# A kernel on one core of a Trainium2 chip: block products of batch 1 in another order, and a last tile in two halves

## The chip, the cores and the metric

The program runs on one core of one Trainium2 chip. The core has five engines that run side by side, each working through its own queue in order: TensorE (PE, matmuls into PSUM), VectorE (DVE), ScalarE (ACT), GpSimd (POOL) and SyncE (SP, which here issues the transfers). PE's granted clock over the profiled execution was 0.994 of full speed. The metric is the device time of one execution in microseconds; the figure given is the median of three runs.

## What is computed

The reference chains three blocks. Attention over clusters makes `x`; a block with a Fourier mix over both axes follows; then a gated block with a convolution along the tokens.

```python
# attention, per batch and head: scores only where q and k fall to the same centroid
x = np.ascontiguousarray(attn_out.transpose(0, 2, 1, 3)).reshape(B, S, H * D)   # 2 x 768 x 512
X = np.fft.fft(np.fft.fft(x, axis=1), axis=2)
u = x + np.real(X)
un = (u - mu) / np.sqrt(var + 1e-06)
u = u + np.maximum(un @ w_ch1, 0.0) @ w_ch2            # 512 -> 2048 -> 512
h = np.maximum(u @ w_in, 0.0)                          # 512 -> 1024
gate = 1.0 / (1.0 + np.exp(-conv_out(h)))              # 3 taps along the tokens
out = h * gate @ w_out                                 # 1024 -> 512
```

The change lies in `np.maximum(un @ w_ch1, 0.0) @ w_ch2` for batch 1, at the start of the gated block, and at the very last output tile.

## The kernel before

The program has three stages: attention with the Fourier mix of batch 0 woven in (to about 225 us), the first feed-forward block (16 weight blocks `f` for each of two batches `g`, to about 497 us), and the gated block (8 weight blocks for each batch, to the end). Every product of the feed-forward blocks is made of three fp16 matmuls (`pass3`, L491 to L494: high by high, high by low, low by high), so each operand is kept as a high and a low half: ACT converts to the high half, DVE subtracts it from the source to get the low half. `general` is the slower variant of the whole program; the run takes the other one, so only lines with `general` false matter.

**Downs.** `downs` (L1834) is a generator: for weight block `f` it multiplies the activated block `h` into six PSUM accumulators, one tile of 128 tokens (three matmuls of 512 columns) per step.

**Batch 1's ups.** For batch 1 the up-products of two weight blocks (a pair `p`) are made by seven block products instead of eight (`ups`, L1729), each of six matmuls of 384 columns: p1, p6, p2, p7, p5, p4, p3 in this order. They need sums of weight quarters, which `weight_sums(p)` (L1714) makes: six additions and subtractions on POOL into the one-buffer tile `sv`, then a conversion on ACT (L1726) and a subtraction on DVE (L1727) into a two-buffer tile. The products' results are added up out of PSUM: ACT copies p1 to `u1` (L1760); DVE adds p6 to give `u2` (L1763), p2 to give half a row `c1` (L1766), p7 to give `u3` (L1769); p5 is copied by ACT to SBUF (L1773), added by DVE to `u3` (L1775, high half of `c2`) and by POOL to `u2`, giving `u4` (L1777); p4 gives the low half of `c2` (L1779), p3 with `u4` the high half of `c1` (L1782). `keep` applies the relu and splits a row in two halves (L1754 on ACT, L1755 on DVE) for a later `downs`.

**Banks.** All these products, and the side work below, are written to the two-buffer PSUM ring `up`: a product can start only when the bank of the last but one has been read out.

**Turns.** `in_turn` lays tiles of downs (d) and products (u) out on PE by a string of letters; a pair's products are spread over two blocks `f`, four in the even one and three in the odd one. The side generator (`gate_in(0)`, L1860) makes batch 0's input of the gated block: per step four transposes, ACT copies (L1906) and a DVE subtraction (L1907), which give the bank back. It is advanced inside `downs` after the tile numbers in `when`.

**Loads.** `load_w` (L728) brings a weight block as raw 64-bit words (a two-buffer tile, 1 MB, issued by SP at L732) and converts it: three DVE steps in a chain, `ops[0]`, `ops[1]`, `ops[3]` (L710, L711, L713), two on ACT (L712, L716), and then squares for the scale on ACT (L759). The gated block's eight blocks b0 to b7 are loaded in this way during batch 1, into slots that batch 1's own blocks leave. `scales("b")` needs all their sums (L772, `sumsb`) before `split_16` (L1681 on ACT, L1682 on DVE) can make fp16 halves of them.

**The order of the queues.** A scheduler lays each engine's instructions out ahead of time: among those that its own model holds ready, the one written first in the program goes first, so one that is ready early may stand ahead of one written earlier. `with tc.issue_after(i):` puts what is issued inside behind instruction `i` in that engine's queue, without a wait for its end.

**The end.** For the last weight block, each of the six output tiles is scaled by DVE or ACT in turn and stored by SP (L1853 to L1857).

Of the kernel before, what the change touches and what calls it, by code (L numbers as in the profile page):

```python
# [449 lines left out]
def tile_net(ctx, tc, qk, v, cen, w12, w34, conv, dft, odd, out, general):  # L450
# [277 lines left out]
    def load_w(k, f):  # L728
# [15 lines left out]
        with tc.issue_after(last_op[0]) if last_op else nullcontext():  # L744
            ops = from64(w, raw, None if general else sums[:, 64 + f:65 + f])
            for op in ops[0:2] + ops[3:4] if not general else ops:
                i = op()
            last_op[:] = [i.ins]
# [963 lines left out]
    sums_w = {}  # L1712

    def weight_sums(p):  # L1714
        k = hp.tile([128, 2048], F32, tag="sv", bufs=1, name=f"sv{p}").rearrange("p (s c n) -> p s c n", s=8, c=2)
        v, a1, a2 = k[:, 0:4], k[:, 4:6], k[:, 6:8]
        for f, d in ((2 * p, a2), (2 * p + 1, a1)):
            w = w32["a", f].rearrange("p (a i h c n) -> p a i h c n", a=2, i=2, h=2, c=2)
            G.tensor_add(d, w[:, 0, 0], w[:, 1, 0])  # L1719
        G.tensor_add(v[:, 0], a2[:, 0], a2[:, 1])  # L1720
        G.tensor_sub(v[:, 1], v[:, 0], a1[:, 0])
        G.tensor_sub(v[:, 2], a1[:, 0], a2[:, 0])
        G.tensor_sub(v[:, 3], a1[:, 1], v[:, 1])
        t = hp.tile([128, 1024], F32, tag="src", bufs=2, name=f"s16{p}").bitcast(F16)
        t = sums_w[p] = t.rearrange("p (a s c n) -> p a s c n", a=2, s=4, c=2)
        A.copy(t[:, 0], v)  # L1726
        V.tensor_sub(t[:, 1], v, t[:, 0])  # L1727

    def ups(p):  # L1729
# [30 lines left out]
        A.copy(u1, o)  # L1760
# [5 lines left out]
        V.tensor_add(c1[:, lo], u1, product("p2", own(0, 1), 1))  # L1766
        yield
        u3 = piece("u3")
        V.tensor_add(u3, u2, product("p7", of_sum(2), 5))  # L1769
        yield  # L1770
        o = product("p5", of_sum(0), 3)
        p5 = piece("p5")
        A.copy(p5, o)  # L1773
        c2 = row(1)
        V.tensor_add(c2[:, hi], u3, o)  # L1775
        u4 = piece("u4")
        G.tensor_add(u4, u2, p5)  # L1777
        yield
        V.tensor_add(c2[:, lo], u3, product("p4", own(1, 1), 6))  # L1779
        keep(c2, 2 * p)  # L1780
        yield
        V.tensor_add(c1[:, hi], u4, product("p3", of_sum(3), 2))  # L1782
# [51 lines left out]
    def downs(s, g, f, side, when=(2,)):  # L1834
# [4 lines left out]
        for t in range(NT):  # L1839
# [4 lines left out]
            if f == last:  # L1844
# [6 lines left out]
                else:  # L1851
                    y = gps[0].tile([128, 512], F32, tag="y", bufs=6, name=f"y{g}{t}")
                    if t % 2:  # L1853
                        V.tensor_scalar(y, acc[s, g][t], yscs[g][:, t:t + 1], None, ALU.mult)
                    else:
                        A.activation(y, acc[s, g][t], AF.Copy, scale=yscs[g][:, t:t + 1])
# [98 lines left out]
    for g in range(B):  # L1955
        for f in range(16):
# [3 lines left out]
            if not general and g == 0 and f > 13:  # L1960
                weight_sums(f - 14)
            if not general and g and f % 2 == 0 and f < 12:
                weight_sums(f // 2 + 2)
            if (g, f) == (B - 1, 15):
                next(side, None)
            steps = downs(0, g, f, side, (1, 4) if g == 0 and f else (2,))
            if not pairs:
                for _ in steps:
                    pass
            elif g == 0:  # L1970
                in_turn(steps, ups(0), iter("ududduuduudud"))
            elif f % 2:
                in_turn(steps, *made)
            else:
                made = (ups(f // 2 + 1), iter("ududdududduddudduddudd")) if f < 14 else ((), repeat("d"))
                in_turn(steps, *made)
            for i in A_LOADS[f] if g == 0 else ():
# [4 lines left out]
            if g == 1 and f in B_LOADS:  # L1982
                load_w("b", B_LOADS.index(f))
# [14 lines left out]
            for i in {13: (0,), 14: (1,), 15: (2,)}.get(f, ()) if g == 1 else ():  # L1998
# [4 lines left out]
    for n in range(-3, 8 * B):  # L2003
        if n + 3 < 8 * B:
            mlp2_up((n + 3) // 8, (n + 3) % 8)
        if 0 <= n + 2 < 8 * B:
# [91 lines left out]
```

## Time and profile before

| | us |
|---|---|
| median of three runs | 638.51 |
| lowest and highest | 636.48, 639.45 |
| the profiled execution | 637.55 |
| its span, first to last instruction | 635.8 |
| PE busy | 602.3 |
| DVE busy | 509.4 |
| ACT busy | 438.2 |
| POOL busy | 236.0 |

The profile shows one execution. The 1.75 us between its time and its span lie outside the first and last instruction. A busy share is a mean over stages; the rows that tell what waits for what come from the waits, which put every idle time of an engine down to the instruction that ended it, and from the timeline, which lists instructions in order with the idle time ahead of them in brackets.

### The profile page before, as it was taken

To read this page: it belongs to the slowest core of one execution; us is meant where nothing else is said; L and a number is where in the kernel's file an instruction comes from. 1 tells how busy PE (TensorE), PEld (TensorE's weight loads), DVE (VectorE), ACT (ScalarE), POOL (GpSimd) and SP (SyncE) were. 2 spreads that over 40 slices of the span, in tenths; PEclk is the share of its full clock that TensorE was granted. 3 is DMA by queue.
4 is the path that set the end of the run, shared out by engine and by line. 5 is a ranking of instruction groups with operands and counts; after the bars stand their busy time and mean duration, and the time that the engine had idled before them with its cause. 6 is when DMAs were issued, how large, how long until landed. Compare 5 with 4: busy or idle time off the path is not lost.

```text
span 635.8 us, 11958 instructions
## 1 busy us (share of the span) xinstructions
PE 602.3 (95%) x4707; PEld 366.7 (58%) x4707; DVE 509.4 (80%) x833; ACT 438.2 (69%) x744; POOL 236.0 (37%) x193
## 2 busy tenths in 40 slices
PE   8899899999999999999999898989999999999995
PEld 4476577676877755566555454544455555555542
DVE  5989979899898898878798298888643799877663
ACT  6788889996889777774678236677511968867652
POOL 4978877875797300001005616445501000000000
PEclk9999999999999999999999999999999999999998
DMA  4776754541310414430432301314200003245202
GB/s 151 206 183 210 210 152 126 155 126 46 100 42 9 195 65 134 142 124 1 147 119 71 129 2 66 133 51 154 96 1 1 1 0 101 101 147 170 81 1 105
DMA packets 21945, 64.41 MB, mean 101 GB/s; under 512 B 7126, under 2 KB 8822, under 8 KB 19064
## 3 DMA queue, kind: packets, MB, share of 16 engines
q1 hardware_dynamic: 20872, 59.81, 29.6%
q0 software_dynamic: 1008, 3.75, 1.9%
q8 instruction: 39, 0.64, 0.4%
q14 instruction: 26, 0.21, 0.1%
HBM read 49.59 MB, written 4.89 MB: 86 GB/s over the span
## 4 chain that ended last, share of the span: by engine, by line
PE 56%; DVE 25%; ACT 12%; issue 3%; DMA 2%; POOL 1%; DVEq 0%; ACTq 0%
PE acc L494 6%; PE acc L493 6%; PE acc L492 6%; PE av L1325 5%; PE t L1269 4%; DVE m6all L1218 4%; PE t L1271 4%; PE s L1209 3%; PE av L1318 2%; PE u L492 2%; PE u L493 2%; PE u L494 2%; PE p L492 2%; DVE wb L711 2%; PE p L493 2%
## 5 line engine op out<-in xcount | busy, mean ns | idle before, releaser
L1306 POOL TENSOR_TENSOR p<-p,p 128x768 f16<-128x768 f32 x61 | 108.1, 1781 | 39.1 <-DVE p L1294 15.0
L1218 DVE TENSOR_REDUCE m6all<-s 128x1 f32<-128x768 f32 x96 | 90.0, 949 | 9.8 <-PE s L1209 7.5
L1278 ACT ACTIVATE p<-t,cbias 128x768 f32<-128x768 f32 x93 | 83.2, 897 | 14.2 <-PE t L1271 13.5
L492 PE MATMUL acc<-wa,h 128*128 128x512 f16 x186 | 70.6, 379 | 0.0
L493 PE MATMUL acc<-wa,h 128*128 128x512 f16 x186 | 70.5, 379 | 0.0
L494 PE MATMUL acc<-wa,h 128*128 128x512 f16 x186 | 70.5, 379 | 0.0
L1325 PEld LDWEIGHTS <-p 128*128 128x128 f16 x1458 | 55.0, 98 | 11.9 <-issue 3.1
L1325 PE MATMUL av<-V,p 128*128 128x65 f16 x1458 | 58.2, 194 | 0.0
L1269 PE MATMUL t<-X 97*128 97x384 f16 x192 | 47.5, 328 | 4.7 <-DVE m6all L1218 2.4
L1209 PE MATMUL s<-X 80*128 80x384 f16 x192 | 46.9, 328 | 5.0 <-DVE eq L1014 3.0
L1296 ACT CAST p<-p 128x768 f16<-128x768 f32 x60 | 49.5, 825 | 0.9
L674 POOL TENSOR_TENSOR rs<-rs,half 128x1 f32<-128x1 f32 x12 | 9.2, 768 | 105.9 <-DVE rs L669 99.7
L1271 PE MATMUL t<-Y 128*128 128x384 f16 x192 | 47.2, 327 | 0.0
L1719 POOL TENSOR_TENSOR sv<-wa 128x512 f32<-128x512 f16 x16 | 26.2, 1657 | 51.7 <-DVE s L1727 37.0
L492 PE MATMUL up<-un,wa 128*128 128x384 f16 x128 | 41.7, 326 | 3.5 <-DVE h L1708 1.9
L492 PE MATMUL u<-x,wb 128*128 128x384 f16 x128 | 41.7, 326 | 1.2 <-DVE h L1803 1.1
L494 PE MATMUL up<-un,wa 128*128 128x384 f16 x128 | 41.7, 326 | 0.0
L493 PE MATMUL up<-un,wa 128*128 128x384 f16 x128 | 41.7, 326 | 0.0
L494 PE MATMUL u<-x,wb 128*128 128x384 f16 x128 | 41.7, 326 | 0.0
L493 PE MATMUL u<-x,wb 128*128 128x384 f16 x128 | 41.7, 326 | 0.0
L493 PE MATMUL acc<-wb,gH 128*128 128x512 f16 x96 | 36.4, 379 | 0.0
L492 PE MATMUL acc<-wb,gH 128*128 128x512 f16 x96 | 36.4, 379 | 0.0
(411 smaller groups left out, 1521.8 us busy)
## 6 DMA issues: line engine op xcount, KB each, us to landing
rawa<-w SPq DMA_DIRECT2D x14, 1024.0 KB
rawb<-w SPq DMA_DIRECT2D x8, 1024.0 KB
heads<-qk SPq DMA_DIRECT2D x8, 768.0 KB
raw<-qk SPq DMA_DIRECT2D x7, 768.0 KB
Y<-G SPq DMA_DIRECT2D x27, 192.0 KB
vraw<-v SPq DMA_DIRECT2D x8, 384.0 KB
heads<-v SPq DMA_DIRECT2D x8, 384.0 KB
out<-y SPq DMA_DIRECT2D x12, 256.0 KB
```

Of the source, the lines that this page charges most:

```text
L492: T.matmul(o, sH, mH, start=start, stop=False)
L493: T.matmul(o, sH, mL, start=False, stop=False)
L494: T.matmul(o, sL, mH, start=False, stop=stop)
L1209: T.matmul(t[:, c, 0:384], X[0:80, 0, sl], X[0:80, 1, 384 * c:384 * c + 384], start=True, stop=True)
L1218: V.tensor_reduce(m6s[h][:, i:i + 1], t[:, :, 0:384], AX.XY, ALU.max, negate=True)
L1269: T.matmul(t[:, c, 0:384], X[0:rx, 1, sl], X[0:rx, 0, 384 * c:384 * c + 384], start=True, stop=False)
L1271: T.matmul(t[:, c, 0:384], Y[0:ry, k, sl], Y[0:ry, q, 384 * c:384 * c + 384], start=False, stop=True)
L1278: A.activation(p, t[:, :, 0:384], AF.Exp, bias=cbias[:, 0:1], scale=0.125 if general else 0.125 / QK_SCALE ** 2)
L1296: A.copy(p16[:, 0], p32s[n])
L1306: eng.tensor_sub(p16[:, 1], p, p16[:, 0])
L1325: T.matmul(o, p16[:, k, 128 * j:128 * j + 128], v16[:, i, h % 2, 65 * part:65 * part + 65], start=(i + j + k + part == 0), stop=(i == 5), ...
L1719: G.tensor_add(d, w[:, 0, 0], w[:, 1, 0])
```

## The change

In short: `weight_sums` loses its conversion and subtraction, which become `split_sums` and are queued behind additions of the pair that is running; both are called behind the downs of a block instead of ahead of them, by two tables of block numbers (16 g + f). The three DVE steps of a load are queued behind `u3`, the high half of `c2` and its low half, by the marks that `ups` had left last when the load was written. The ACT copy of p5, `u4` and POOL's addition are gone; DVE adds p5 to `u2` in place. `u3` is kept in the high half of `c1`. The turns of pair 0 and the side step's places change. The third weight block of the gated block is split behind its first up-product. The last output tile is scaled in two halves, one by DVE and one by ACT, and stored by two issues, one from SP and one from ACT.

```diff
@@ load_w
-            for op in ops[0:2] + ops[3:4] if not general else ops:
-                i = op()
+            if general:
+                for op in ops:
+                    i = op()
+            else:
+                for op, m in ((ops[0], "u3"), (ops[1], "c2"), (ops[3], "c2lo")):
+                    with tc.issue_after(marks[m]):
+                        i = op()
@@ weight sums
-    sums_w = {}
+    sums_w, marks = {}, {}
+    SUM_SPLITS = {14: (0,), 15: (1,), **{2 * p + 12: (p,) for p in range(2, 8)}}
+    WEIGHT_SUMS = {12: (0,), 14: (1,), 15: (2,), **{2 * p + 10: (p,) for p in range(3, 8)}}
+
+    def split_sums(p):
+        v = sums_w[p][:, 0:4]
         t = hp.tile([128, 1024], F32, tag="src", bufs=2, name=f"s16{p}").bitcast(F16)
         t = sums_w[p] = t.rearrange("p (a s c n) -> p a s c n", a=2, s=4, c=2)
-        A.copy(t[:, 0], v)
-        V.tensor_sub(t[:, 1], v, t[:, 0])
+        with tc.issue_after(marks["u1"]) if p == 1 else nullcontext():
+            A.copy(t[:, 0], v)
+        with tc.issue_after(marks["c1"]) if marks else nullcontext():
+            V.tensor_sub(t[:, 1], v, t[:, 0])
@@ ups
-        u3 = piece("u3")
-        V.tensor_add(u3, u2, product("p7", of_sum(2), 5))
+        u3 = c1[:, hi]
+        marks["u3"] = V.tensor_add(u3, u2, product("p7", of_sum(2), 5)).ins
         yield
         o = product("p5", of_sum(0), 3)
-        p5 = piece("p5")
-        A.copy(p5, o)
         c2 = row(1)
-        V.tensor_add(c2[:, hi], u3, o)
-        u4 = piece("u4")
-        G.tensor_add(u4, u2, p5)
+        marks["c2"] = V.tensor_add(c2[:, hi], u3, o).ins
+        V.tensor_add(u2, u2, o)
         yield
-        V.tensor_add(c2[:, lo], u3, product("p4", own(1, 1), 6))
+        marks["c2lo"] = V.tensor_add(c2[:, lo], u3, product("p4", own(1, 1), 6)).ins
         keep(c2, 2 * p)
         yield
-        V.tensor_add(c1[:, hi], u4, product("p3", of_sum(3), 2))
+        V.tensor_add(c1[:, hi], u2, product("p3", of_sum(3), 2))
@@ the last output tile
+                    if (g, t) == (B - 1, NT - 1) and not general:
+                        V.tensor_scalar(y[:, 0:256], acc[s, g][t][:, 0:256], yscs[g][:, t:t + 1], None, ALU.mult)
+                        A.activation(y[:, 256:512], acc[s, g][t][:, 256:512], AF.Copy, scale=yscs[g][:, t:t + 1])
+                        nc.sync.dma_start(out=out[g, 128 * t:128 * t + 128, 0:256], in_=y[:, 0:256])
+                        nc.scalar.dma_start(out=out[g, 128 * t:128 * t + 128, 256:512], in_=y[:, 256:512])
+                        yield
+                        continue
@@ the loop over g and f
-            if not general and g == 0 and f > 13:
-                weight_sums(f - 14)
-            if not general and g and f % 2 == 0 and f < 12:
-                weight_sums(f // 2 + 2)
-            steps = downs(0, g, f, side, (1, 4) if g == 0 and f else (2,))
+            when = (1, 4) if g == 0 and f else (2,) if general or not g else (3,) if f % 2 else (5,)
+            steps = downs(0, g, f, side, when)
-                in_turn(steps, ups(0), iter("ududduuduudud"))
+                in_turn(steps, ups(0), iter("uduududuududd"))
+            for p in SUM_SPLITS.get(16 * g + f, ()) if not general else ():
+                split_sums(p)
+            for p in WEIGHT_SUMS.get(16 * g + f, ()) if not general else ():
+                weight_sums(p)
-            for i in {13: (0,), 14: (1,), 15: (2,)}.get(f, ()) if g == 1 else ():
+            for i in {13: (0,), 14: (1,), 15: (2,) if general else ()}.get(f, ()) if g == 1 else ():
@@ the gated block's loop
+        if n == -3 and not general:
+            ws_b[2] = split_16(wbp[0], "b", 2)
```

## Rows read from the trace of the kernel before

**Rows 1.** The page, part 1: busy us, share of the span, instructions.

```profile
PE 602.3 (95%) x4707; PEld 366.7 (58%) x4707; DVE 509.4 (80%) x833; ACT 438.2 (69%) x744; POOL 236.0 (37%) x193
```

**Rows 2.** PE's waits, 345 to 490 us: total us, times, longest.

```profile
PE p L492 <- DVE u L1763: 4.5, 3, 1.8
PE p L492 <- DVE x L1907: 2.4, 3, 1.5
PE up L492 <- DVE h L1708: 1.9, 1, 1.9
```

**Rows 3.** PE's waits, 490 to 520 us.

```profile
PE u L492 <- DVE h L1803: 1.1, 1, 1.1
```

**Rows 4.** DVE's timeline, pairs 2 to 4: start, duration, instruction, [idle before].

```profile
394.36 2.18 DVE L711 SCALAR_TENSOR_TENSOR wb<-rawb,wb 128x1024 int32<-128x1024 int32 x1
396.46 0.54 DVE L1763 TENSOR_TENSOR u<-u,p 128x384 f32<-128x384 f32 x1
...
402.49 1.23 DVE L711 SCALAR_TENSOR_TENSOR wb<-rawb,wb 128x1024 int32<-128x1024 int32 x1
...
407.92 0.68 DVE L1907 TENSOR_TENSOR x<-xT,x 128x512 f16<-128x512 f32 x1
...
430.43 0.69 DVE L710 TENSOR_SCALAR wb<-rawb 128x1024 int32<-128x1024 int32 x1 [0.50 <-DMA rawb<-w]
...
436.34 1.19 DVE L710 TENSOR_SCALAR wb<-rawb 128x1024 int32<-128x1024 int32 x1 [0.30 <-PE acc L494]
```

**Rows 5.** POOL's timeline, first two weight sums for pairs 2 and 4.

```profile
358.38 2.26 POOL L1719 TENSOR_TENSOR sv<-wa 128x512 f32<-128x512 f16 x2 [2.42 <-DVE s L1727]
...
393.65 3.90 POOL L1719 TENSOR_TENSOR sv<-wa 128x512 f32<-128x512 f16 x2 [6.06 <-DVE s L1727]
```

**Rows 6.** ACT's timeline, pair 1's conversion.

```profile
355.99 1.05 ACT L1726 CAST s<-sv 128x1024 f16<-128x1024 f32 x1 [4.72 <-POOL sv L1723]
```

**Rows 7.** Stretches, pairs 2 and 7: length, busy PE, PEld, DVE, ACT, POOL.

```profile
390.00:408.20 18.20, 15.96 (x89) 8.61 (x88) 15.43 (x18) 12.44 (x25) 8.92 (x7) 1.00 0.33 116
...
475.00:490.00 15.00, 15.00 (x84) 8.09 (x82) 5.16 (x8) 2.92 (x5) 0.99 (x1) 1.00 0.01 1
```

**Rows 8.** PE's timeline, end of pair 2.

```profile
405.45 0.60 PE L1904 MATMUL xT<-ident,U 128*128 128x128 f32 x4
405.89 0.38 PE L492 MATMUL acc<-wa,h 128*128 128x512 f16 x1
...
406.53 0.33 PE L492 MATMUL p<-un,s 128*128 128x384 f16 x1
...
407.51 0.38 PE L492 MATMUL acc<-wa,h 128*128 128x512 f16 x1
...
408.80 0.33 PE L492 MATMUL p<-un,wa 128*128 128x384 f16 x1
```

**Rows 9.** Groups by line: busy us, mean ns | idle before.

```profile
L1777 POOL TENSOR_TENSOR u<-u,p 128x384 f32<-128x384 f32 x8 | 10.0, 1254 | 43.8 <-ACT p L1773 43.7
...
L1769 DVE TENSOR_TENSOR u<-u,p 128x384 f32<-128x384 f32 x8 | 4.4, 551 | 4.2 <-PE p L494 4.2
```

**Rows 10.** The chain that ended last, in order of time: a raw transfer.

```profile
425.68 4.73 DMA rawb<-w
```

**Rows 11.** ACT's timeline, the last square of b6.

```profile
443.75 0.19 ACT L759 ACTIVATION_READ_ACCUMULATOR rawb<-wb 128x1 f32 x1
```

**Rows 12.** ACT's and DVE's timelines, start of the gated block.

```profile
500.69 1.93 ACT L1681 ACTIVATE wb<-wb,scb 128x512 f16<-128x512 f32 x3
...
500.86 1.40 DVE L1682 SCALAR_TENSOR_TENSOR wb<-wb,scb,wb 128x512 f16<-128x512 f32 x2
502.19 0.55 DVE L1809 SCALAR_TENSOR_TENSOR h<-u,x 128x384 f32<-128x384 f32 x1
```

**Rows 13.** DVE's and SP's timelines, the end.

```profile
628.69 0.75 DVE L1854 TENSOR_SCALAR y<-acc,ysc 128x512 f32<-128x512 f32 x1 [0.54 <-PE acc L494]
...
626.16 3.64 SPq L1857 DMA_DIRECT2D out<-y  x6
```

More of the change, by code (lines that the diff above doesn't have):

```diff
@@ L1710, in mlp1_up @@
             ws[0, g, f + 1] = split_16(hp, "a", f + 1)
-    sums_w = {}
+    sums_w, marks = {}, {}
+    SUM_SPLITS = {14: (0,), 15: (1,), **{2 * p + 12: (p,) for p in range(2, 8)}}
+    WEIGHT_SUMS = {12: (0,), 14: (1,), 15: (2,), **{2 * p + 10: (p,) for p in range(3, 8)}}
     def weight_sums(p):
-        k = hp.tile([128, 2048], F32, tag="sv", bufs=1, name=f"sv{p}").rearrange("p (s c n) -> p s c n", s=8, c=2)
+        k = sums_w[p] = hp.tile([128, 2048], F32, tag="sv", bufs=1, name=f"sv{p}").rearrange("p (s c n) -> p s c n", s=8, c=2)
         v, a1, a2 = k[:, 0:4], k[:, 4:6], k[:, 6:8]
@@ L1759, in ups @@
         u1 = piece("u1")
-        A.copy(u1, o)
+        marks["u1"] = A.copy(u1, o).ins
         yield
@@ L1765, in ups @@
         c1 = row(0)
-        V.tensor_add(c1[:, lo], u1, product("p2", own(0, 1), 1))
+        marks["c1"] = V.tensor_add(c1[:, lo], u1, product("p2", own(0, 1), 1)).ins
         yield
-        u3 = piece("u3")
-        V.tensor_add(u3, u2, product("p7", of_sum(2), 5))
+        u3 = c1[:, hi]
+        marks["u3"] = V.tensor_add(u3, u2, product("p7", of_sum(2), 5)).ins
         yield
         o = product("p5", of_sum(0), 3)
-        p5 = piece("p5")
-        A.copy(p5, o)
         c2 = row(1)
-        V.tensor_add(c2[:, hi], u3, o)
-        u4 = piece("u4")
-        G.tensor_add(u4, u2, p5)
+        marks["c2"] = V.tensor_add(c2[:, hi], u3, o).ins
+        V.tensor_add(u2, u2, o)
         yield
-        V.tensor_add(c2[:, lo], u3, product("p4", own(1, 1), 6))
+        marks["c2lo"] = V.tensor_add(c2[:, lo], u3, product("p4", own(1, 1), 6)).ins
         keep(c2, 2 * p)
         yield
-        V.tensor_add(c1[:, hi], u4, product("p3", of_sum(3), 2))
+        V.tensor_add(c1[:, hi], u2, product("p3", of_sum(3), 2))
         keep(c1, 2 * p + 1)
@@ L1982, in tile_net @@
             if g == 1 and f in B_LOADS:
-                load_w("b", B_LOADS.index(f))
+                for i in range(8):
+                    if B_LOADS[i] == f:
+                        load_w("b", i)
             if (g, f) == (0, 14):
```

## The prediction

> **What bounds the kernel now.** I read the page's busy times first: TensorE (PE) is busy 602.3 of 635.8 us [rows 1], so an edit on another engine pays only where it ends a wait of PE. I then read PE's waits over the stage that the diff touches, from the last up-products of batch 0's loop to the end of batch 1's pairs (345 to 490 us) [rows 2]. There are seven, all on a PSUM bank of the two-buffer `up` ring that an engine has not read out: 4.5 us in three for the addition to `u2` (L1763), 2.4 us in three for the low half of a transposed block (L1907), 1.9 us in one for L1708. Together 8.8 us. After 490 us there is one more, 1.1 us [rows 3]. That is all the change can win on PE, besides the tail behind the last matmul.
>
> The timelines show why they arise. In pair 2, VectorE (DVE) starts L711 of a weight load at 394.36 and holds it 2.18 us; `u2`'s addition is behind it at 396.46, and p2, whose bank it frees, waits with PE idle: the longest of the three, 1.8 us [rows 2, 4]. L711 took 1.23 us at 402.49, with GpSimd (POOL) idle for most of it; the 2.18 us lie beside POOL's first two sums, which took 3.90 us there and 2.26 at 358.38 [rows 4, 5]. So two engines slow each other, and DVE's order puts the slowed instruction in front of an addition that PE needs. The 1.9 us wait is another order: ScalarE (ACT) sits 4.72 us at L1726 until POOL has summed pair 1's weights [rows 6], with the reading out of `up` queued behind it.
>
> DVE is not short of time on average: 15.43 of 18.20 us in pair 2, 5.16 of 15.00 in pair 7, which has neither loads nor weight sums [rows 7].
>
> **Clock of a pair.** From PE's starts in pair 2: a tile of three downs is 0.65 us (407.51 to 408.80 for two), a product 0.98 (406.53 to 407.51), a block of transposes 0.44 (405.45 to 405.89, where the next downs stand) [rows 8]. Twelve tiles, seven products and two blocks are 15.5 us. In the new turns, counted from p1's start: p1 0, p6 1.6, p2 3.9, p7 5.5, first transposes 7.8, p5 8.2, p4 10.5, second transposes 12.8, p3 13.2, next p1 15.5.
>
> **The change part by part.**
> *Weight sums and splits.* For pair 1 the ACT copy and DVE subtraction go behind `u1` and `c1` of pair 0, whose operands PE makes; L1708 then waits for PE alone. The 1.9 us go. What is added to pair 0 is one subtraction of 1024 columns (an estimated 1.2 us, since 384 took 551 ns [rows 9]), needed only at p6 of pair 1, some 8 us later; if that cover were gone it would cost its own length. For the other pairs the subtraction goes from ahead of `u2` to behind `c1` (about 5.5), and ends at 6.8, before p7's result needs DVE.
>
> *Loads.* Each load's three DVE steps are pinned: L710 behind `u3` (7.2), L711 behind `c2`'s high half, L713 behind its low half. Nothing of a load stands ahead of `u2` or `c1` any more unless the last L713 is very late; so the 4.5 us go. The order also spreads the loads: before, a load started when its slot came free and pair 2 held two; now pairs 1 to 5 hold one each, pair 6 two, pair 7 one. DVE loses about (15.43 - 5.16)/2 = 5.1 us at most from pair 2. Who waits behind L710: `c2`'s additions, L711, L713, then ACT's L712, L716 and L759 and, on SP's queue, the transfer that reuses the raw buffer. The transfer takes 4.73 us [rows 10]; a raw buffer is refilled a pair ahead, so that is hidden, except for the last three.
>
> *Side step.* The transposes go behind d5 and d3. Their bank is next wanted by p4 (2.7 us after the first block) and the next p1 (2.3 us after the second); before, p2 and p7 stood 0.65 us and one product behind. The 2.4 us go for the first block. For the second, DVE has L711, `c2`'s low half, L713, the relu's low half and L1907 (0.68 us [rows 4]) in 5 us. No row of before has that order: the bounds are 0 (before's second blocks showed no wait; at 408.80 p1 started without one [rows 8]) and 1.5 us a pair (the longest L1907 wait [rows 2]). I take 0.4, nearer the row of the same block, in pairs 2 to 4: 1.2 us given back.
>
> *Additions.* The ACT copy of p5 and POOL's addition (1254 ns) go; DVE gets one addition like L1769's, 551 ns [rows 9], behind `c2`'s high half. It frees p5's bank at about 10.4, and that bank is wanted at 12.8: nothing on PE's path. `u3` in `c1`'s high half moves no time.
>
> By the Trainium skill, SBUF — State Buffer, "Who interferes with whom", a DVE instruction with two SBUF inputs and a POOL instruction take turns on a shared port, and the second to issue fully blocks. Here the rows agree in size: 0.95 us more for L711 and 1.64 us more for POOL's two sums. The rule speaks against the change in that POOL's sums now start at about 6.8 us, right under L710 and L711; what it makes of the time is rival A.
>
> *The last loads.* b5 and b6 sit in pair 6, b7 behind `u3` of pair 7. b6's chain took from 436.34 (L710) to 443.94 (its last square), 7.6 us [rows 4, 11]. From 7.2 of pair 7 that ends at 14.8, and the sums over all squares are due on PE when pair 7's downs end, at 14.6 (no transposes there). Bounds 0 and 3 us (two more DVE steps ahead of it, or a raw transfer that ends late); I take 0.6, since b6's row is the nearest.
>
> *Second stage's start.* The third `wb` split goes behind the first up-product. Before, two L1682 (1.40 us) stood ahead of L1809 at 502.19, the wait of rows 3. But ACT is full there as well (three L1681 at 500.69, 1.93 us, ahead of the second read-out) [rows 12], and the gate chain behind it, not PE, releases the first down-product. So between 0 and 1.1 us; I take 0.2.
>
> *Last tile.* DVE's scale of 512 columns ends the compute, 628.69 to 629.44, then SP issues [rows 13]. 384 columns took 551 ns [rows 9], so 256 take an estimated 0.4: 0.35 us sooner. The second half goes out by ACT's queue, which issues no DMA in this trace; bounds: half of the SP row's 3.64/6 = 0.6 us gained (0.3), or a completion of its own that costs up to 1 us more. I take 0.35 in all.
>
> By the Trainium skill, DMA: Bandwidth & Descriptors, "Issuing engines are not separate DMA queues", a second queue saves only the issuing time. By it the tail gains the 0.35 us of compute and no more, which is what I took.
>
> **The sum.** 8.8 + 0.2 + 0.35 - 1.2 - 0.6 = 7.5 us; 0.2 more for pairs 5 and 6, where copies of `cb` and two loads stand in place of a block: 7.3. The profiled execution took 637.55 us (span 635.8 plus 1.75 around it), so it would be 630.2. It lies 0.96 us under the median of 638.51, so against the median I forecast 631.2.
>
> **Rivals.**
> A. *The waits move to the second half of the pair.* POOL's sums start at 6.8, and the first two of six alone took 2.26 to 3.90 us [rows 5]. L711 from 10.4 then ends at 12.6 instead of 11.6, `c2`'s low half at 13.1, L713, slowed by half as much as L711, at an estimated 14.8, then the relu's low half (768 columns, an estimated 0.9 from rows 9) and L1907 at 16.4: next p1 stalls up to 0.9 us in each of four or five pairs, some 4 us with what p3 loses. With 2 us at the last loads the gain falls to 9.35 - 6 = 3.3: 635.2. For: the 2.18 and 3.90 us [rows 4, 5]. Against: DVE holds one load fewer.
> B. *The pins don't change what PE waits for.* The waits were on slow DVE instructions, and the scheduler puts others in the holes: only the 1.9 us go and half of it comes back: 637.5. Against: the three L1763 waits each have one load step directly ahead.
> C. *Slower: DVE's queue blocks at L710.* It stands in an in-order queue behind `u3` and needs its raw data. Before, DVE waited 0.50 us for raw data at 430.43, behind a 4.73 us transfer [rows 4, 10]. L710 (1.19 us at 436.34) and L1907 (0.68) must both end before p4 at 10.5, so L710 has 1.4 us of slack. Were every transfer to start only when `u3` is due, each of eight loads would lose 3.3 us, 27 against 9.35 gained: about 656. It decides from raw data landing 2.6 us behind `u3`, where the loss per load (1.2 us) eats the gain. Against: a raw buffer is free half a pair earlier.
> D. *Nothing new waits*: the whole 8.8, 1.1 and 0.4: 628.2.
>
> **How the numbers follow.** Forecast 0.50, A 0.20, B 0.09, C 0.06, D 0.15. About 0.5% (3.2 us) is what a measurement of this kernel can tell from no change, so the line lies at 635.3. Faster: forecast, D and 0.12 of A, 0.77. Same: the rest of A and B, 0.17. Slower: C, 0.06. The range takes in D with 0.6 us of scatter and most of A, up to a gain of 2: 627.6 to 636.5.
>
> **What would show it.** Right: PE's waits between 345 and 490 us fall from 8.8 to about 2 us, none of them on `u2`; L1726 no longer has 4.7 us of waiting on POOL ahead of L1708; what is left names L1907 or `c2`. If A holds, L711 and L713 keep about 1.8 us and PE waits before p1 or p3. If C holds, DVE shows idle on a DMA before L710. The step at the last loads is wrong if PE idles on the sums behind pair 7. The forecast falls altogether if additions still sit behind L711 or L713.

## The result, and the profile after

The changed kernel takes 628.93 us (median; 627.59 to 629.37) against 637.69 us for the kernel before on the same chip (636.48 to 639.45): a ratio of 0.9857, 95% interval 0.9827 to 0.9887, so 1.1 to 1.7% faster. The forecast was 631.2 us, with 627.6 to 636.5 as its range. The profiled execution took 629.05 us with a span of 627.3; the one of before took 637.55 with 635.8. The two spans differ by 8.5 us.

TensorE's busy time and share in the page after, to be read beside [rows 1]:

```profile
PE 599.8 (96%) x4707; PEld 365.7 (58%) x4707; DVE 513.2 (82%) x841; ACT 433.2 (69%) x737; POOL 226.0 (36%) x185
```

The instructions are nearly the same and VectorE has more to do than before. What changed is what TensorE waits for. Its waits after, from 345 to 490 us, and the first of those from 490 to 520 us (tile, line, what it waited for: us in total, times, longest):

```profile
PE acc L494 <- DVE h L1767: 0.3, 1, 0.3
```

```profile
PE u L492 <- DVE h L1818: 0.7, 1, 0.7
```

Against [rows 2] the 8.8 us in seven waits have become 0.3 us in one, and the wait of [rows 3] went from 1.1 to 0.7. Lines have moved: `u2`'s addition is L1775 now (was L1763), the low half of a transposed block L1923 (L1907), the activations' second half L1713 (L1708), ScalarE's half of the split L1737 (L1726).

VectorE's timeline of pair 2 (start, duration, line, tile, and in brackets the idle time before it with what ended it). It is the pair in which [rows 4] showed L711 ahead of `u2`:

```profile
392.88 0.56 DVE L1775 TENSOR_TENSOR u<-u,p 128x384 f32<-128x384 f32 x1
394.49 0.56 DVE L1778 TENSOR_TENSOR uc<-u,p 128x384 f32<-128x384 f32 x1 [1.05 <-PE p L494]
394.96 1.22 DVE L1739 TENSOR_TENSOR s<-sv,s 128x1024 f16<-128x1024 f32 x1
396.11 0.55 DVE L1781 TENSOR_TENSOR uc<-u,p 128x384 f32<-128x384 f32 x1
396.58 1.44 DVE L710 TENSOR_SCALAR wb<-rawb 128x1024 int32<-128x1024 int32 x1
...
399.99 1.49 DVE L711 SCALAR_TENSOR_TENSOR wb<-rawb,wb 128x1024 int32<-128x1024 int32 x1
401.41 0.54 DVE L1788 TENSOR_TENSOR uc<-uc,p 128x384 f32<-128x384 f32 x1
401.87 1.29 DVE L713 SCALAR_TENSOR_TENSOR wb<-rawb,wb 128x1024 uint32<-128x1024 uint32 x1
```

`u2` (L1775) and `c1` (L1778) have nothing long ahead of them; the split, L710, L711 and L713 stand each behind the addition that the change names. The long waits are now VectorE's own, on TensorE. ScalarE's row ahead of pair 0 shows the same for the split: L1711, the activations' first half, waits for TensorE alone, where [rows 6] had 4.72 us on GpSimd with L1708's read-out behind it:

```profile
357.17 0.49 ACT L1711 ACTIVATE h<-up 128x384 f16<-128x384 f32 x1 [5.27 <-PE up L494]
```

**Stalls that the list of waits leaves out.** A matmul of 512 columns has a row of 0.38 us, but the next one starts 0.21 to 0.22 us later; with 384 columns the row is 0.33 and the step 0.16. So a stall of up to 0.16 us lies under the row of the matmul ahead of it, and each listed wait is 0.16 us too short. TensorE's timeline after, at the end of pair 2:

```profile
404.67 0.38 PE L494 MATMUL acc<-wa,h 128*128 128x512 f16 x1
405.09 0.32 PE L492 MATMUL p<-un,wa 128*128 128x384 f16 x1
405.25 0.32 PE L493 MATMUL p<-un,wa 128*128 128x384 f16 x1
```

From 404.67 to 405.09 is 0.42 us where 0.22 is the rule: p1 of the next pair started 0.2 us late, and no view lists it. I added up, over TensorE's starts from 345 us to the end of the pairs, all that goes beyond the ordinary step (0.216 and 0.163 us; 0.43 between transposes and a product; what is under 0.08 is left out). Before: 10.5 us. After: 1.4. The sum follows the measured times of the kernels here (e6 and e8, which are not in the table, lose 1.4 us as the changed kernel does):

| kernel | lost in TensorE's starts, us | time, us |
|---|---|---|
| before | 10.5 | 637.7 |
| changed | 1.4 | 628.93 |
| e10, additions alone | 16.4 | 644.44 |
| e1, loads not pinned | 7.7 | 634.53 |
| e9, L711 twice | 7.2 | 634.77 |
| e12, first pin alone | 7.0 | 634.31 |
| e4, old additions | 6.2 | 632.65 |
| e7, before without sums | 5.4 | 632.31 |
| e2, old sums | 3.5 | 631.32 |
| e5, pins alone | 3.4 | 630.64 |
| e3, old side steps | 1.6 | 628.80 |
| e11, changed without sums | 0.0 | 626.76 |

Against the changed kernel, lost starts and time differ by the same amount to within 1.1 us in every row. The lost starts are those of the profiled execution and the times are medians; against the profiled times the two agree to within 1.0 us, but for e9 (5.8 us of starts, 4.2 us of time), where 1.2 us of the difference lie ahead of the pairs: their first product starts at 362.23 us there and at 363.39 in the changed kernel. So nearly the whole effect is in the pairs, and the rest of the change moves little.

### The profile page after: what moved, and what is told of

The parts are those of the page before. It is cut to its first block, busy times and chain, and to the rows that moved or that the text cites. A ratio compares the mean times of both kernels' runs of the same rounds, so it can differ in the third digit from the quotient of the medians.

```text
span 627.3 us, 11929 instructions
## 1 busy us (share of the span) xinstructions
PE 599.8 (96%) x4707; PEld 365.7 (58%) x4707; DVE 513.2 (82%) x841; ACT 433.2 (69%) x737; POOL 226.0 (36%) x185
## 4 chain that ended last, share of the span: by engine, by line
PE 60%; DVE 24%; ACT 10%; issue 3%; POOL 1%; DMA 1%; DVEq 0%; ACTq 0%
PE acc L494 6%; PE acc L493 6%; PE acc L492 6%; PE av L1330 5%; DVE m6all L1223 4%; PE t L1274 4%; PE t L1276 4%; PE s L1214 3%; PE av L1323 2%; PE p L492 2%; PE u L492 2%; PE p L494 2%; PE p L493 2%; PE u L494 2%; PE u L493 2%
## 5 line engine op out<-in xcount | busy, mean ns | idle before, releaser
L1311 POOL TENSOR_TENSOR p<-p,p 128x768 f16<-128x768 f32 x61 | 108.6, 1790 | 39.5 <-DVE p L1299 16.4
L1726 POOL TENSOR_TENSOR sv<-wa 128x512 f32<-128x512 f16 x16 | 21.7, 1377 | 70.5 <-DVE s L1739 55.8
```

Of the source, the lines that this page charges most:

```text
L1311: eng.tensor_sub(p16[:, 1], p, p16[:, 0])
```

## Experiments

Each time is a median; the ratio is to the kernel before on the same chip (637.43, 637.77 and 638.44 us in the three groups e1 to e4; e5, e6, e7 and e9; e8 and e10 to e12).

### e1: the changed kernel, loads not pinned

```
-                for op, m in ((ops[0], "u3"), (ops[1], "c2"), (ops[3], "c2lo")):
-                    with tc.issue_after(marks[m]):
-                        i = op()
+                for op in ops[0:2] + ops[3:4]:
+                    i = op()
```

> The changed kernel with the three pins of a load taken away; all else stays. Theory 1 (queue order: what PE waited for was load steps standing ahead of additions on DVE): most of the 4.5 us of waits on u2 or like additions come back, 3 to 6 us in all, 632 to 635 us. Theory 2 (contention: POOL's sums at their old place made the load steps long, and the new place cures it): under 1 us, about 629.5. Theory 3 (distance: the side step's new place gives the banks time): under 1 us as well.

Measured: 634.53 us, ratio 0.9951 (0.9936 to 0.9966). TensorE's largest group of waits, 345 to 490 us:

```profile
PE p L492 <- DVE x L1922: 4.2, 5, 1.5
```

5.6 us come back, so the pins carry most of the gain. But they come back on the transposed block (L1922), though its new turns are kept, and only 0.3 us on the addition of p6 that gives `u2`: the waits go to whatever stands behind L711, and that has changed with the rest of the order.

### e2: the changed kernel, weight sums and splits at their old place

```
-        with tc.issue_after(marks["u1"]) if p == 1 else nullcontext():
-            A.copy(t[:, 0], v)
-        with tc.issue_after(marks["c1"]) if marks else nullcontext():
-            V.tensor_sub(t[:, 1], v, t[:, 0])
+        A.copy(t[:, 0], v)
+        V.tensor_sub(t[:, 1], v, t[:, 0])
...
+            if not general and g == 0 and f > 13:
+                weight_sums(f - 14)
+                split_sums(f - 14)
+            if not general and g and f % 2 == 0 and f < 12:
+                weight_sums(f // 2 + 2)
+                split_sums(f // 2 + 2)
...
-            for p in SUM_SPLITS.get(16 * g + f, ()) if not general else ():
-                split_sums(p)
-            for p in WEIGHT_SUMS.get(16 * g + f, ()) if not general else ():
-                weight_sums(p)
```

> The changed kernel with POOL's weight sums and their conversion and subtraction written where the kernel before has them (ahead of the downs, no pins on them). Theory 1: the 1.9 us ahead of pair 0 come back and little else, PE waits of 2 to 2.5 us, about 631. Theory 2: the load steps are long again where they meet the sums, 4 to 7 us, 633 to 636. Theory 3: as theory 1.

Measured: 631.32 us, ratio 0.9914 (0.9889 to 0.9938). The largest group of waits, 345 to 490 us:

```profile
PE up L492 <- DVE h L1713: 1.9, 1, 1.9
```

The 1.9 us of [rows 2] are back as they were, with 0.8 us in two others beside them: 2.4 us in time. This step of the prediction stands.

### e3: the changed kernel, side steps at their old turns

```
-            when = (1, 4) if g == 0 and f else (2,) if general or not g else (3,) if f % 2 else (5,)
+            when = (1, 4) if g == 0 and f else (2,)
```

> The changed kernel with the side step of batch 1's blocks behind tile 2, as before. Theory 3: the 2.4 us of waits on the transposed block's low half come back, and u2's too since a bank less is free between p6 and p2: 2.4 to 7 us, 631.5 to 636. Theory 1: with the loads pinned nothing long stands ahead of these, under 1 us, 629 to 630.

Measured: 628.80 us, ratio 0.987 (0.9842 to 0.9897); waits on the transposed block 0.4 us in two. The new distance between transposes and the next product is worth nothing that can be measured once the loads are pinned. The prediction gave this step the 2.4 us of L1907; that was wrong, as e1 shows too: with the new turns and no pins, 4.2 us of waits stand on that block.

### e4: the changed kernel, p5 copied by ScalarE and added by GpSimd

```
+        p5 = piece("p5")
+        A.copy(p5, o)
         marks["c2"] = V.tensor_add(c2[:, hi], u3, o).ins
-        V.tensor_add(u2, u2, o)
+        u4 = piece("u4")
+        G.tensor_add(u4, u2, p5)
...
-        V.tensor_add(c1[:, hi], u2, product("p3", of_sum(3), 2))
+        V.tensor_add(c1[:, hi], u4, product("p3", of_sum(3), 2))
```

> The changed kernel with p5 copied by ACT and added to u2 on POOL again (u4), as before. All three theories: p5's bank is wanted 2.4 us later, so PE waits stay under 1 us and the time within 0.5 us of the changed kernel's, 628.5 to 629.5. A rival holds that the POOL addition, queued with the weight sums and needed by c1's high half, delays them: 1 to 3 us more.

Measured: 632.65 us, ratio 0.9926 (0.9902 to 0.9951). The largest group of TensorE's waits, 345 to 490 us; then GpSimd's last sum and its addition, and VectorE's addition for `c1`, at the end of pair 1:

```profile
PE p L492 <- DVE uc L1794: 4.7, 5, 1.1
```

```profile
388.49 1.59 POOL L1730 TENSOR_TENSOR sv<-sv 128x256 f32<-128x256 f32 x1
390.04 1.71 POOL L1789 TENSOR_TENSOR u<-u,p 128x384 f32<-128x384 f32 x1
```

```profile
391.79 0.56 DVE L1794 TENSOR_TENSOR uc<-u,p 128x384 f32<-128x384 f32 x1 [0.89 <-POOL u L1789]
```

The edit is worth 3.7 us where the prediction had nothing. GpSimd now makes its sums in the second half of the pair, its addition is queued behind them, and `c1`'s high half (L1794) waits for that while it holds the bank that the next product wants, about 1 us in each of five pairs.

### e10: the kernel before, with the additions edit alone

```
-        p5 = piece("p5")
-        A.copy(p5, o)
         c2 = row(1)
         V.tensor_add(c2[:, hi], u3, o)
-        u4 = piece("u4")
-        G.tensor_add(u4, u2, p5)
+        V.tensor_add(u2, u2, o)
...
-        V.tensor_add(c1[:, hi], u4, product("p3", of_sum(3), 2))
+        V.tensor_add(c1[:, hi], u2, product("p3", of_sum(3), 2))
```

> The kernel before with the additions edit alone: ScalarE's copy of p5 and GpSimd's addition are gone, VectorE adds p5 into u2 out of the accumulation bank. Loads, sums and splits stand where they did. Theory 1 (the prediction: nothing on TensorE's path, the edit is only worth something where GpSimd's queue holds the moved sums): the waits of 8.8 us in the stretch from 345 to 490 us stay within 1 us, time 636.5 to 638. Theory 2 (the addition through GpSimd also costs the kernel before, where the sums run ahead of it): the waits fall by 2 to 4 us, time 633.5 to 635.5 us. Theory 3 (0.55 us more of VectorE per pair in front of late conversions): waits grow by 0.5 us in three to five pairs, 639 to 640 us.

Measured: 644.44 us, ratio 1.0104 (1.0084 to 1.0125): slower by 6 us. Theory 3 has the sign, and less than half of the size. The largest group of waits, 345 to 490 us; VectorE ahead of the longest of them; and three windows, each beginning 1.0 to 1.3 us behind the end of one of those waits (start and end, length, busy of TensorE, its weight loads, VectorE, ScalarE and GpSimd, then the granted clock, the DMA share and GB/s):

```profile
PE p L492 <- DVE u L1763: 7.5, 3, 3.1
```

```profile
394.06 1.65 DVE L710 TENSOR_SCALAR wb<-rawb 128x1024 int32<-128x1024 int32 x1
395.74 2.05 DVE L711 SCALAR_TENSOR_TENSOR wb<-rawb,wb 128x1024 int32<-128x1024 int32 x1
397.72 0.54 DVE L1763 TENSOR_TENSOR u<-u,p 128x384 f32<-128x384 f32 x1
```

```profile
399.30:402.50 3.20, 3.20 (x10) 1.35 (x9) 1.32 (x3) 2.74 (x7) 2.18 (x3) 0.50 0.00 0
419.60:422.70 3.10, 3.10 (x11) 1.33 (x10) 1.08 (x2) 2.47 (x6) 1.92 (x3) 0.51 0.00 0
457.00:460.00 3.00, 3.00 (x18) 1.56 (x16) 0.99 (x2) 2.44 (x6) 1.87 (x3) 1.00 0.00 0
```

In the kernel before, L710 of this load stood ahead of the relu's low half (L1755), and L711 alone between that and `u2`:

```profile
391.38 0.69 DVE L710 TENSOR_SCALAR wb<-rawb 128x1024 int32<-128x1024 int32 x1
...
393.49 0.95 DVE L1755 SCALAR_TENSOR_TENSOR h<-uc,h 128x768 f16<-128x768 f32 x1
```

The edit names no load, but with it the scheduler lays L710 out behind L1755. There it runs beside GpSimd's sums, takes 1.65 us, and both it and L711 (2.05) stand ahead of `u2`: the wait grows from 1.8 to 3.1 us. All waits together (7.5 here, 1.9 on L1708, 1.8 and 0.3 on two others) go from 8.8 to 11.5 us. The rest of the 6 us is the clock: behind the waits of 3.06 and 2.19 us TensorE ran 3.2 and 3.1 us at a granted clock of 0.50 and 0.51, that is at 1.2 GHz, and the steps between its starts were twice as long. The third wait, of 2.24 us, was followed by no such stretch. 2.7 us of waits and about 3.1 us of slow starts make 5.8.

### e5: the kernel before, with the pins alone

```
-            for op in ops[0:2] + ops[3:4] if not general else ops:
-                i = op()
...
+                for op, m in ((ops[0], "u3"), (ops[1], "c2"), (ops[3], "c2lo")):
+                    with tc.issue_after(marks[m]):
+                        i = op()
...
```

> The kernel before with one part of the change alone: the three conversions of each load of batch 1's second weight are placed behind the additions u3, c2 high half and c2 low half. Weight sums, splits, additions through GpSimd, side steps and the last tile stay as before. Theory 1 (VectorE's queue order): the 4.5 us on u2 and the 2.4 us on the transposed block vanish, the 1.9 us on the activations of the old split (L1708) stay, and the addition that GpSimd makes after the sums still ends late, which the run with the old additions priced at 3.9 us in the new order of the sums: 631 to 634 us. Theory 2 (contention: the conversions are long because GpSimd's sums run beside them, and the order is second): the sums run on, so more than half of the 4.5 us comes back somewhere: 635 to 638 us. Rival: the pins are only worth anything together with the moved sums: 637 to 638 us.

Measured: 630.64 us, ratio 0.9888 (0.9873 to 0.9903). Waits, 345 to 490 us:

```profile
PE up L492 <- DVE h L1713: 1.9, 1, 1.9
PE p L492 <- DVE u L1768: 0.4, 1, 0.4
```

Pins alone bring 7.1 us. They end the waits on the transposed block and all but 0.4 us of those on `u2`; the 1.9 us stay, as theory 1 said. The time is a little better than that theory's 631 to 634: with the sums still early, TensorE has no wait on GpSimd's addition. Put together with e2 and e4: on top of the pins, the moved sums alone cost 2.0 us (e4, 632.65), the additions edit alone changes nothing that can be told (e2, 631.32, in an interval that overlaps this one; lost starts of 3.5 and 3.4 us), both together bring 1.7 (628.93). Side steps, third split and tail are in those figures, and are worth nothing measurable (e3, e6, e8). The turns of pair 0 are in them too, and no run takes these back; in the kernel before, TensorE's starts lost 0.2 us in pair 0 and at the start of pair 1, which bounds what the new turns can win there.

### e12: the changed kernel with the first pin alone

```
-                for op, m in ((ops[0], "u3"), (ops[1], "c2"), (ops[3], "c2lo")):
-                    with tc.issue_after(marks[m]):
+                for op, m in ((ops[0], "u3"), (ops[1], None), (ops[3], None)):
+                    with tc.issue_after(marks[m]) if m else nullcontext():
```

> The changed kernel with only the first conversion of each load (L710) held back behind u3; L711 and L713 are no longer held behind c2's two halves. Theory 1 (the first place is the one that counts: it takes the whole load away from u2): 629 to 630.5 us, TensorE waits under 1.5 us more in all. Theory 2 (each place counts: L711 and L713, 2.7 us together, stand in front of c2's high half and of the additions behind it, and the second transposes and p3 come late): 1 to 2 us in each of four or five pairs, 633 to 636 us.

Measured: 634.31 us, ratio 0.9937 (0.9919 to 0.9955); theory 2. It is no better than no pin at all (e1). The largest group of waits, and VectorE in pair 2 behind L710:

```profile
PE p L492 <- DVE x L1923: 3.0, 5, 0.7
```

```profile
398.52 2.06 DVE L711 SCALAR_TENSOR_TENSOR wb<-rawb,wb 128x1024 int32<-128x1024 int32 x1
400.50 0.68 DVE L1923 TENSOR_TENSOR x<-xT,x 128x512 f16<-128x512 f32 x1
```

L711 follows L710 at once, and the transposed block whose bank p4 wants stands behind it. So, with the sums moved, holding back L710 alone is worth nothing; the places of L711 and L713 are needed. Whether these two would do without L710's, no run shows.

### e7: the kernel before, without GpSimd's sums from pair 3 on

```
+        if p > 2:
+            v = sums_w["kept"]
...
+            A.copy(t[:, 0], v)
+            V.tensor_sub(t[:, 1], v, t[:, 0])
+            return
...
+        sums_w["kept"] = v
```

> The kernel before, but GpSimd makes no weight sums from pair 3 on: the sums of pair 2 are split again for each later pair, so part of the products is that of other weights. All orders of VectorE's and ScalarE's queues stay. Theory 1 (order): the waits of TensorE on u2 (4.5 us in three) stay, shorter by what the conversions gain without GpSimd beside them, about 0.9 us each at most: 1.8 to 4 us left, and the wait of 1.9 us at pair 2's sums stays as it is; time 633 to 636 us. Theory 2 (contention): conversions take 0.7 to 1.25 us instead of up to 2.18, and the waits on u2 vanish (under 0.5 us in all); time 630 to 632.5 us. GpSimd's own addition for c1 comes early in both, so that the wait on the transposed block falls in both.

Measured: 632.31 us, ratio 0.9918 (0.9903 to 0.9933); theory 2, with 0.8 us on `u2` where it said under 0.5. L711 from 345 to 490 us, first in the kernel before, then here (line, operation, tile, shapes, count | busy, mean ns | idle before), and TensorE's waits on `u2` here:

```profile
L711 DVE SCALAR_TENSOR_TENSOR wb<-rawb,wb 128x1024 int32<-128x1024 int32 x8 | 13.9, 1738 | 0.2
```

```profile
L711 DVE SCALAR_TENSOR_TENSOR wb<-rawb,wb 128x1024 int32<-128x1024 int32 x8 | 9.8, 1222 | 0.2
```

```profile
PE p L492 <- DVE u L1771: 0.8, 3, 0.3
```

VectorE's order is unchanged, instruction by instruction, and the waits on `u2` fall from 4.5 to 0.8 us; 1.9 us on L1708 stay, and 1.0 on the transposed block. L711 is 0.5 us shorter on average, and ScalarE and VectorE no longer wait for late sums either, which this run doesn't separate. So the waits of before needed both, the place and the stretching: take either away and most of them are gone (e5, e7). The two gains don't add.

### e11: the changed kernel, without GpSimd's sums from pair 3 on

```
-        k = sums_w[p] = hp.tile([128, 2048], F32, tag="sv", bufs=1, name=f"sv{p}").rearrange("p (s c n) -> p s c n", s=8, c=2)
+        k = sums_w[p] = sums_w["kept"] if p > 2 else hp.tile([128, 2048], F32, tag="sv", bufs=1, name=f"sv{p}").rearrange("p (s c n) -> p s c n", s=8, c=2)
...
+        if p > 2:
+            sums_w[p] = sums_w["kept"]
+            return
+        sums_w["kept"] = k
```

> The changed kernel, but GpSimd makes no weight sums from pair 3 on: the sums of pair 2 are split again for each later pair, so part of the products is that of other weights. It takes the contention out of the changed kernel as an earlier run took it out of the kernel before (there 638 to 632.3 us). Theory 1 (order and contention are each enough: with the loads behind the additions the stretching of L710 from 0.69 to 1.4 us falls into slack): within 0.7 us of the changed kernel, 628.2 to 629.6 us, conversions shorter by 0.5 to 0.8 us per load all the same. Theory 2 (the contention that is left still costs): 626 to 627.5 us.

Measured: 626.76 us, ratio 0.982 (0.9802 to 0.9837); theory 2 by the time. TensorE has no wait over the listing's threshold between 345 and 490 us, and its lost starts go from 1.4 us to none. The three conversions in the changed kernel, and here:

```profile
L711 DVE SCALAR_TENSOR_TENSOR wb<-rawb,wb 128x1024 int32<-128x1024 int32 x8 | 11.0, 1380 | 0.1
L713 DVE SCALAR_TENSOR_TENSOR wb<-rawb,wb 128x1024 uint32<-128x1024 uint32 x8 | 10.5, 1310 | 0.0
L710 DVE TENSOR_SCALAR wb<-rawb 128x1024 int32<-128x1024 int32 x8 | 8.5, 1064 | 0.0
```

```profile
L711 DVE SCALAR_TENSOR_TENSOR wb<-rawb,wb 128x1024 int32<-128x1024 int32 x8 | 9.8, 1221 | 0.1
L713 DVE SCALAR_TENSOR_TENSOR wb<-rawb,wb 128x1024 uint32<-128x1024 uint32 x8 | 9.8, 1219 | 0.0
L710 DVE TENSOR_SCALAR wb<-rawb 128x1024 int32<-128x1024 int32 x8 | 5.5, 686 | 0.0
```

Contention in the changed kernel is 0.16 us on L711, 0.09 on L713 and 0.38 on L710, on average; it has moved to L710, which the prediction did not count among the slowed. What it costs on TensorE is 1.4 us. The time fell by 2.2 us; of the 2.1 us by which the last scaling comes earlier in the profile, 0.7 lie ahead of 357 us, where both kernels are the same.

### e9: the changed kernel with L711 issued twice

```
-                for op, m in ((ops[0], "u3"), (ops[1], "c2"), (ops[3], "c2lo")):
+                for op, m in ((ops[0], "u3"), (ops[1], "c2"), (ops[1], "c2"), (ops[3], "c2lo")):
```

> The changed kernel with the second conversion of each load (L711, behind c2's high half) issued twice with the same result: eight times 1.25 to 1.5 us more of VectorE work between c2's high and low halves, in front of the second transposes and p3. Slack theory of the prediction (VectorE has about 1 us to spare there, second transposes wait 0.4 us per pair already): 1 to 1.5 us of TensorE waits per load in pairs 2 to 5, 4 to 6 us in all, 633 to 635 us. Theory 2 (the measured waits are near nothing since VectorE is well over 1.5 us ahead there): under 1 us in all, 628.5 to 629.5 us.

Measured: 634.77 us, ratio 0.9951 (0.9935 to 0.9966): 5.8 us lost, as the slack theory said. The three largest groups of waits:

```profile
PE p L492 <- DVE uc L1788: 2.0, 1, 2.0
PE p L492 <- DVE x L1923: 1.7, 2, 0.9
PE p L492 <- DVE uc L1791: 0.8, 1, 0.8
```

At the second transposes (L1923) and the next product (L1791) the 1.3 us that were added show as 0.8 to 0.9 of waiting in each of three pairs. So VectorE had at most about half a microsecond to spare there. The 2.0 us are one wait in pair 5, where both L711 stand ahead of `c2`'s low half (L1788):

```profile
450.24 2.94 DVE L711 SCALAR_TENSOR_TENSOR wb<-rawb,wb 128x1024 int32<-128x1024 int32 x2
```

Rival A was near: the changed kernel has nearly used up what it won on that engine.

### e6 and e8: the last tile whole; the third split at its old place

```
-                    if (g, t) == (B - 1, NT - 1) and not general:
+                    if False:
```

> The changed kernel with the last output tile scaled by one VectorE instruction and stored by one transfer, as before the change. Theory of the prediction (halves overlap, 0.35 us gained): from the start of the last tile's scaling to the end of the span about 7.75 us, against 7.4 in the changed kernel; time 0.35 us more, 629.2. Theory 2 (the two halves read one accumulation bank one after the other, and the second store starts later than one whole store would): 7.1 us as in the kernel before, time 0.3 us less, 628.5. Either difference is below what the times can tell; the span from the last scaling to the end decides.

```
-            for i in {13: (0,), 14: (1,), 15: (2,) if general else ()}.get(f, ()) if g == 1 else ():
+            for i in {13: (0,), 14: (1,), 15: (2,)}.get(f, ()) if g == 1 else ():
...
-        if n == -3 and not general:
-            ws_b[2] = split_16(wbp[0], "b", 2)
```

> The changed kernel with the third split of the second stage's weights at its old place, one step earlier, ahead of the last products' activations. Theory 1 (the new place takes the split out from in front of the first activations of the second stage): the wait of TensorE on VectorE's h at the start of the second stage grows from 0.7 to about 1.15 us as in the kernel before, time 0.3 to 0.5 us more, 629.2 to 629.5 us. Theory 2 (it makes no difference): 628.9 us. The times can hardly tell them apart; the wait in the trace does.

Measured: 629.45 us (0.9859, 0.984 to 0.9878) and 629.31 us (0.986, 0.9838 to 0.9882): neither differs from the changed kernel. The last tile in the changed kernel, then in e6:

```profile
619.88 0.48 DVE L1863 TENSOR_SCALAR y<-acc,ysc 128x256 f32<-128x256 f32 x1 [0.54 <-PE acc L494]
620.39 0.47 ACT L1864 ACTIVATE y<-acc,ysc 128x256 f32<-128x256 f32 x1 [0.48 <-DVE y L1863]
620.49 0.55 SPq L1865 DMA_DIRECT2D out<-y  x1
620.90 0.39 ACTq L1866 DMA_DIRECT2D out<-y  x1
```

```profile
620.51 0.75 DVE L1870 TENSOR_SCALAR y<-acc,ysc 128x512 f32<-128x512 f32 x1 [0.54 <-PE acc L494]
```

ScalarE's half does not run beside VectorE's: it waits 0.48 us for it, and so its store is issued at 620.90, 1.0 us behind the start of the scaling. From that start to the end of the span are 7.4 us in the changed kernel (619.88 to 627.3), 7.2 in e6 (620.51 to 627.7) and 7.1 before (628.69 [rows 13] to 635.8). Over all fourteen traces of this case the stretch is 6.8 to 7.8 us with a whole tile (five kernels) and 7.2 to 8.0 with halves (nine). So the halves gain nothing that shows, and the 0.2 to 0.3 us that they lose in the first three figures lie within the scatter. In e8 the wait at the start of the second stage is

```profile
PE u L492 <- DVE h L1812: 1.3, 1, 1.3
```

against 0.7 in the changed kernel, and the span is 627.2 against 627.3. The new place takes 0.6 us from that wait, and the end does not come sooner by an amount that these runs can tell.

## Why the prediction came out as it did

The direction and the mechanism hold: TensorE waited for additions queued behind slow VectorE instructions and for one read-out queued behind a wait on GpSimd, and the new order ends these waits. The size of the gain lies between the forecast and rival D: 7.3 us were forecast, D had 10.3 (638.51 to 628.2), and 8.5 are shown by the spans, 8.8 by the medians. That the time itself, 628.93, looks nearer to D's 628.2 than to the forecast's 631.2 comes in part from the kernel before, whose median is 0.8 us lower here than the one that the forecast started from. D's own condition, that nothing new waits, does not hold: 1.4 us were lost anew. Term by term:

- **8.8 us of waits removed: right, and 1.7 too small.** The listed waits leave out what lies under the row ahead. By TensorE's starts the pairs lost 10.5 us before.
- **Pins, 4.5 us: too small.** Alone they bring 7.1 us: they end nearly all of the 4.5 us on `u2` and also the 2.4 us on the transposed block, which the prediction gave to the side steps (e3, e5). And in the new order of the sums L710's place alone is worth nothing; those of L711 and L713 are needed (e12).
- **Sums and splits, 1.9 us: right** (e2), but not free on the other side: they push GpSimd's queue into the second half of the pair.
- **Additions, "nothing on PE's path": the step that failed.** I looked at the bank that p5 holds, and not at GpSimd's queue, where the addition would have stood behind the moved sums. Beside the moved sums the edit is worth 3.7 us (e4); in the old order it costs 6, about half of it by the clock (e10). The forecast took no harm from it, because the changed kernel has the new addition, and there it is hidden as the prediction said; but of what the edit is for it had no account.
- **Second blocks and next p1, 1.2 us given back: 1.4 measured, and the agreement is luck.** At the place that the term names, the next p1 behind pairs 2 to 4, 0.1 to 0.2 us were lost each time, 0.5 in all. Another 0.7 were lost at the start of pair 2 (389.88 to 391.05), where the listed wait names the low half of a relu of pair 1 (L1767) and neither L1923 nor `c2`, and 0.1 within a pair. e9 shows the slack as small as the prediction had it, and e11 that GpSimd's sums use it up.
- **Last loads, 0.6 us, and pairs 5 and 6, 0.2 us: nothing lost.** The last load's L710 ran at 473.18 in 0.69 us, GpSimd being done, and TensorE shows no stall on the sums.
- **Second stage, 0.2 us gained: about 0.** The first wait fell from 1.1 to 0.7 us, but other stalls take its place: from the start of batch 1's last down-product (497.38 us before, 488.52 after) to that of the last scaling are 131.31 us before and 131.36 after.
- **Last tile, 0.35 us gained: no gain,** and 0.3 lost in these two profiled executions. The step assumed that both engines read the tile at once. By the Trainium skill, PSUM — Partial Sum Buffer, "PSUM bank collisions raise a hardware error", the compiler's scheduler adds a dependency between any two instructions on different engines that touch the same bank and the same quadrant of partitions. The trace agrees: the halves are columns of one accumulation tile, and ScalarE's waited 0.48 us for VectorE's. They also write one output tile `y`, and no run here shows which of the two tiles made ScalarE wait.

With these the account closes. TensorE's lost starts fall by 10.5 - 1.4 = 9.1 us in the pairs, and its last down-product there starts 8.9 us sooner; less 0.05 in the second stage and 0.3 in the tail this is 8.5 us, as the spans have it.

**Rivals.** B falls: the pins do change what TensorE waits for. C falls: L710 waits for no transfer (idle before it 0.0 us in the changed kernel's row above). A was right that the sums start under L710 and L711 (396.32 us, 7.6 us into the pair), and wrong in the price: L711 took 1.3 to 1.6 us in pairs 1 to 5, not 2.18, and L710 1.4 in pairs 2 to 5.

**Contention.** GpSimd's rows beside the load of pair 2:

```profile
396.32 2.72 POOL L1726 TENSOR_TENSOR sv<-wa 128x512 f32<-128x512 f16 x2 [6.61 <-DVE s L1739]
398.99 0.73 POOL L1727 TENSOR_TENSOR sv<-sv 128x256 f32<-128x256 f32 x1
399.68 0.73 POOL L1729 TENSOR_TENSOR sv<-sv 128x256 f32<-128x256 f32 x1
400.36 1.73 POOL L1728 TENSOR_TENSOR sv<-sv 128x256 f32<-128x256 f32 x1
```

A sum of 256 columns takes 0.73 us beside additions that read one operand from PSUM and 1.73 beside L711, and L710, 0.69 us alone, takes 1.44 beside the first sums. By the Trainium skill, SBUF — State Buffer, "Who interferes with whom", not only an instruction with two SBUF inputs but also a `tensor_scalar` in a two-port mode takes the port that GpSimd needs, and the one that issues second waits for the other's end. The rows agree that L710, which has one input, is slowed; that it runs in that mode no run here shows, though alone it takes 0.69 us where L711, with two inputs, takes 1.22 for as many columns (e11).

## What to carry to other kernels

Before costing an edit at nothing, write down for every engine what will be queued ahead of the edited instruction in the new order, not in the old one: the same addition was worth 3.7 us in one order and cost 6 in the other, where it moved a load that it does not name. When a wait has two causes in series (a slowed instruction, and its place ahead of an urgent one), either cure takes most of the gain, so cures must not be added up. And judge a tight loop by the steps between TensorE's starts: what lies under the overlap of two matmuls is in no list, 0.16 us of each wait that is listed and all of a shorter one, and here it made 1.7 us of 10.5.

## What was not expected of the hardware

- Two waits of TensorE, of 3.06 and 2.19 us, were followed by stretches of 3.2 and 3.1 us at a granted clock of 0.50 (1.2 GHz), so that these waits cost 1.5 and 1.7 times their own length; a third wait of 2.24 us was followed by 1.00. What tells them apart stays open.
- A VectorE instruction with a single SBUF input (L710) was stretched from 0.69 to 1.44 us beside GpSimd.
- Two engines scaling two halves of one accumulation bank into one output tile took turns: 0.48 us of waiting for 0.47 us of work. Which of the two tiles forced the turns stays open.
